# Two-layer decode block on one core: a tile per half of wq, second-layer softmax ahead of the key turns, value steps re-spaced, last values loaded into key tiles

## The chip, the cores and the metric

The kernel runs on one core of a Trainium2 chip. The metric is the time of one execution on the device in microseconds (us); a profile of one execution gives its span, which is about 1.8 us shorter than the time. The engines are PE (matrix multiply, TensorE), DVE (VectorE), ACT (ScalarE) and SP, which here only issues transfers. All loads go through one queue and are spread over 16 DMA engines.

A run is called fast or slow by its time: slow means over 1.5% above the fastest run of the same kernel. Ratios below are the mean time of one kernel's fast runs over that of the kernel before's fast runs of the same rounds, so they are not quite the ratios of the medians that are quoted with them. Microseconds worked out from a ratio are (1 - ratio) x 374.8.

## The reference

Batch 4, one new token each, model width 512. A grouped-query attention block (32 query heads, 8 key/value heads, 4096 cached keys, head size 128) and a gated feed-forward block (width 1792) are applied twice, with the **same** weights and the **same** caches both times:

```python
x = A_x
x = x + _A_ref(_layernorm(x), k_cache, v_cache, wq, wo)
x = x + _B_ref(_layernorm(x), w_gate, w_up, w_down)
x = x + _A_ref(_layernorm(x), k_cache, v_cache, wq, wo)
x = x + _B_ref(_layernorm(x), w_gate, w_up, w_down)
# _A_ref: q = x @ wq; p = softmax(q k^T / sqrt(128)); (p v) @ wo
# _B_ref: (gelu(x @ w_gate) * (x @ w_up)) @ w_down
```

All inputs are bf16. Keys and values of one batch entry are 8.4 MB each.

## The kernel before

A batch entry's keys are loaded once, as 16 tiles of 512 KB (`KT`), and serve both layers. A tile has to be transposed by DVE once (a "key turn"). Values are not kept: they are streamed once for each layer through a ring of six slots of 512 KB. So block b does: scores of layer 2 for entry b-1 from the keys that are still there; each key tile is then free and is loaded with entry b's keys; softmax of layer 2 (two head groups); key turns; scores and softmax of layer 1 for entry b; 16 value steps of layer 1; output projection; the dense stage (feed-forward, next queries) into which the 16 value steps of layer 2 for entry b-1 are woven. One value step is 16 matmuls on one value tile, and it frees the tile's slot.

```python
KV_BUFS = 6
wq_sb = wts.tile([P, KD, HqDh], BF16, name="wq_sb")         # both head groups in one tile
KT = [[wts.tile([P, CH, Dh], BF16, ...) for t in range(NT)] for i in range(Hkv)]

def load_v(upto):                                            # values go through the ring alone
    while seen["load"] < min(upto * VB, seen["use"] + KV_BUFS):
        ...
        v = kvin.tile([P, CH, Dh], BF16, name="v_t", tag="kv")
        dq.dma_start(out=v[:], in_=cache_tile(A_v_cache, plan[i][0], kvh, t))

# in attend(b2, b1), blocks two to four:
for g in range(NG):
    for t in range(NT):
        scores(sc2[g], g, t)
        keys.load(GH)
p0 = soft(sc2[0]); build_q1(b1, 0)
turn()                                                       # waits for the first key tile
z0 = soft_turn(*p0); prob2[0] = (soft_swap(p0[0], p2p), z0)
p0 = soft(sc2[1]); build_q1(b1, 1)
turn()
z0 = soft_turn(*p0); prob2[1] = (soft_swap(p0[0], p2p), z0)
turn(2)
# ... 5 more turns and the first score half ...
turn(2); vals.step(2); sc1 = new_scores(); scores(sc1, 1, 0)
turn(4); vals.step(2); scores(sc1, 1, 1); vals.step(2)       # and so on
# (cut: dense(), attend_last(), the first block)
```

An instruction that waits holds up what stands behind it in the program on the same engine: in the trace below, one wait of 15.1 us on PE holds up all later matmuls, and the key turns on DVE with them.

Of the kernel before, what the change touches and what calls it, by code (L numbers as in the profile page):

```python
# [29 lines left out]
def kernel(  # L30
# [50 lines left out]

    dq = nc.sync

    wq_sb = wts.tile([P, KD, HqDh], BF16, name="wq_sb")
    wo_sb = wts.tile([P, Hq, D], BF16, name="wo_sb")
    wg_sb = wts.tile([P, KD, F], BF16, name="wg_sb")
    wu_sb = wts.tile([P, KD, F], BF16, name="wu_sb")
# [26 lines left out]

    def load_wq(g):
        n = HG * Dh
        dq.dma_start(out=wq_sb[:, :, g * n:(g + 1) * n], in_=wq_dram[:, :, g * n:(g + 1) * n])

    def load_rest():
        n = Hq // 4  # L120
# [72 lines left out]
    def turn_rows(rows, n):  # L193
        t = tmpp.tile([P, n // QS, QS], FP32, name="rt", tag="row")
        nc.vector.transpose(out=t.rearrange("p n j -> p (n j)"), in_=rows[:, :n])  # L195
        return t

    def q_rows(b0, nb, g):
        bs = slice(b0, b0 + nb)
        rows = new_rows()  # L200
        for k in range(KD):
            for j in range(QD):
                n0 = (g * GH + j) * rep * Dh
                w = wq_sb[:, k, n0:n0 + rep * Dh].rearrange("p (m i e) -> p m e i", i=QS, e=2)
                nc.tensor.matmul(rows[j * QS:j * QS + nb, :], lhsT=xn_bf[:, k, bs], rhs=w,  # L205
                                 start=(k == 0), stop=(k == KD - 1))
        return rows
# [27 lines left out]
    def build_q1(b, g):  # L235
        q_build(q_spread(q1_bf[:, g, :, b], amask, g), g)


    def y_select(rows, nb):
        t = turn_rows(rows, 512).rearrange("p (k a) j -> p a k j", a=QD)  # L240
        y = ps_sm.tile([P, KD, nb], FP32, name="y", tag="sm")
        for a in range(QD):
            nc.tensor.matmul(y[a * QS:(a + 1) * QS], lhsT=s32_f[:, :], rhs=t[:, a, :, :nb],
                             start=True, stop=True)
        return y
# [57 lines left out]
    class Keys:  # L303
# [14 lines left out]
        def turn(self, count=1):  # L318
            for _ in range(count):
                kvh, t = self.tile(self.nt)  # L320
                self.nt += 1
                words = KT[kvh][t].rearrange("p c d -> p (c d)").bitcast(FP32)
                nc.vector.transpose(out=words, in_=words)  # L323
# [33 lines left out]
    def soft_turn(pp, ls):  # L357
        flat = pp.rearrange("p c j -> p (c j)")
        nc.vector.transpose(out=flat, in_=flat)  # L359
        zx = zp.tile([P, GH, rep], FP32, name="zx", tag="zx")  # L360
        nc.vector.tensor_scalar(out=zx[:], in0=dmask[:], scalar1=ls[:, 0:1], scalar2=None,
                                op0=ALU.mult)
        return zx
# [18 lines left out]
    ring = []  # L382
    seen = {"load": 0, "use": 0}

    def load_v(upto):
        while seen["load"] < min(upto * VB, seen["use"] + KV_BUFS):
            i, n = divmod(seen["load"], VB)
            seen["load"] += 1
            kvh, t = divmod(n, NT)
            v = kvin.tile([P, CH, Dh], BF16, name="v_t", tag="kv")  # L390
            dq.dma_start(out=v[:], in_=cache_tile(A_v_cache, plan[i][0], kvh, t))
            ring.append(v)

# [35 lines left out]
    def attend(b2, b1):  # L429
        two, first = b2 is not None, b1 == 0  # L430
        prob1, prob2 = {}, {}
        keys = Keys(b1)
        turn = keys.turn
        vals = Values(b1, 0, prob1, lambda k: OT_bf[:, k * rep:(k + 2) * rep],
                      1 if first else len(plan))
        if two:
            sc2 = [new_scores() for g in range(NG)]
            for g in range(NG):
                for t in range(NT):
                    scores(sc2[g], g, t)  # L440
                    keys.load(GH)
            p0 = soft(sc2[0])
            build_q1(b1, 0)
            turn()
            z0 = soft_turn(*p0)
            prob2[0] = (soft_swap(p0[0], p2p), z0)
            p0 = soft(sc2[1])
            build_q1(b1, 1)
            turn()
            z0 = soft_turn(*p0)  # L450
            prob2[1] = (soft_swap(p0[0], p2p), z0)
            turn(2)
        else:
            load_wq(0)
            keys.load(TG)
            load_wq(1)
            keys.load(TG)
            load_v(1)
            make_identity(nc, ident_bf[:])
            build_consts()  # L460
            xT_ps = ps_sm.tile([P, KD, B], BF16, name="xT_ps", tag="sm")
            for k in range(KD):
                nc.tensor.transpose(xT_ps[:, k, :], x_bf[:B, k * P:(k + 1) * P], ident_bf[:B, :B])
            nc.vector.tensor_copy(out=XX[:, 0].rearrange("p b k -> p k b"), in_=xT_ps[:])
            ln_square(0, B)
            rstd1 = ln_rstd(B, ln_center(0, B))
            q_first(q_rows(0, B, 0), 0, rstd1)
            build_q1(0, 0)
            turn(4)
        sc1 = new_scores()  # L470
        scores(sc1, 0, 0)
        turn(4)
        scores(sc1, 0, 1)
        if first:
            q_first(q_rows(0, B, 1), 1, rstd1)
            build_q1(0, 1)
        turn()
        p0 = soft(sc1)
        turn()
        z0 = soft_turn(*p0)  # L480
        prob1[0] = (soft_swap(p0[0], p1p), z0)
        turn(2)
        vals.step(2)
        sc1 = new_scores()
        scores(sc1, 1, 0)
        turn(4)
        vals.step(2)
        scores(sc1, 1, 1)
        vals.step(2)
        p0 = soft(sc1)  # L490
        vals.step()
        z0 = soft_turn(*p0)
        vals.step()
        prob1[1] = (soft_swap(p0[0], p1p), z0)
        rows = new_rows()
        hp = 2 * rep
        if first:
            vals.step(TG)
            load_rest()
            load_v(len(plan))  # L500
            out_proj(rows, OT_bf, 0, Hq)
        else:
            for i in range(2):
                vals.step()
                out_proj(rows, OT_bf, i * hp, hp)
            vals.step(3)
            out_proj(rows, OT_bf, 2 * hp, hp)
            vals.step(3)
            out_proj(rows, OT_bf, 3 * hp, hp)
        assert vals.n == VB  # L510
        return rows, prob2

    def attend_last(b2):
        prob2 = {}
        vals = Values(b2, 1, prob2, lambda k: OT2_bf[:, k * rep:(k + 2) * rep, b2])
        sc2 = [new_scores() for g in range(NG)]
        for g in range(NG):
            for t in range(NT):
                scores(sc2[g], g, t)
        for g in range(NG):  # L520
            p0 = soft(sc2[g])
            z0 = soft_turn(*p0)
            prob2[g] = (soft_swap(p0[0], p2p), z0)
            vals.step(2)
        vals.step(6)
        rows = new_rows()
        hp = 2 * rep
        for i in range(2):
            vals.step()
            out_proj(rows, OT2_bf, i * hp, hp)  # L530
        vals.step(3)
        out_proj(rows, OT2_bf, 2 * hp, hp)
        vals.step(3)
        out_proj(rows, OT2_bf, 3 * hp, hp)
        return rows

    def dense(b0, nb, rows, fill):
        y = y_select(rows, nb)
        fill(2)
        add_y(b0, nb, y)  # L540
        ln_square(b0, nb)
        mv = ln_center(b0, nb)
        fill(1)
        rg = ffn_in(b0, nb, wg_sb)
        rstd = ln_rstd(nb, mv)
        sq, h = gelu(nb, rg, rstd)
        ru = ffn_in(b0, nb, wu_sb)
        H_bf = gate_up(nb, sq, h, ru)
        fill(3)
        y = y_select(down(nb, H_bf), nb)  # L550
        add_y(b0, nb, y)

    x_bf = tmpp.tile([P, D], BF16, name="x_bf", tag="row")
# [3 lines left out]
    for b in range(B):  # L557
        fill = (lambda n: None) if prev is None else prev.step
        dense(b, 1, rows, fill)
        fill(2)  # L560
        ln_square(b, 1)
        mv = ln_center(b, 1)
        fill(2)
        rstd = ln_rstd(1, mv)
        am = small.tile([P, QD], FP32, name="am", tag="am")
        nc.vector.tensor_scalar(out=am[:], in0=amask[:], scalar1=rstd[:, 0:1], scalar2=None,
                                op0=ALU.mult)
        qr = [q_rows(b, 1, g) for g in range(NG)]
        for g in range(NG):
            qm = q_spread(turn_rows(qr[g], 512)[:, :, 0], am, g)  # L570
            fill(2)
            q_build(qm, g)
        fill(VB)
        if b < B - 1:
            rows, prob2 = attend(b, b + 1)
            prev = Values(b, 1, prob2, lambda k, b=b: OT2_bf[:, k * rep:(k + 2) * rep, b])
        else:
            rows = attend_last(b)
# [41 lines left out]
```

## Time and profile before

374.75 us, median of three runs (373.92 to 376.08). The page of the profiled run, first its busy line, then, of the rows in 40 equal slices, the mean busy share of the DMA engines in tenths and what they moved, then the load queue's packets, bytes and share:

```profile
PE 216.0 (58%) x3522; PEld 114.2 (31%) x3522; DVE 173.5 (46%) x476; ACT 24.2 (6%) x54; POOL 0.7 (0%) x6
...
DMA  7999428999929969998999599899993999996900
GB/s 277 398 409 406 192 99 304 372 366 386 390 88 368 410 233 343 359 322 299 337 407 410 180 300 396 299 336 354 413 409 129 333 384 356 319 339 180 375 17 0
...
q1 hardware_dynamic: 35744, 114.58, 83.7%
```

The kernel moves 114.6 MB. Its best slices run at 405 to 413 GB/s, at which these bytes would take about 280 us (worked out: 114.6 MB / 0.41 MB per us). The other 95 us are slices in which the queue moves less. No engine that computes is near full over the span. The Trainium skill, "Perfetto Trace Analysis", Roofline, says that a lone core's HBM rate is bounded by its 16 DMA engines at about 435 GB/s.

Windows of the trace in which the queue had little it was allowed to fetch (window, its length, busy time of each engine, granted clock, DMA busy share, GB/s):

```profile
42.00:53.00 11.00, 3.26 (x63) 2.41 (x67) 9.53 (x17) 2.65 (x4) 0.00 (x0) 0.63 0.03 9
104.00:110.00 6.00, 4.57 (x62) 1.71 (x58) 3.07 (x9) 0.00 (x0) 0.00 (x0) 0.81 0.05 17
206.00:212.00 6.00, 3.30 (x62) 2.23 (x65) 6.00 (x9) 1.00 (x3) 0.00 (x0) 0.50 0.23 87
282.00:288.00 6.00, 3.03 (x62) 2.17 (x65) 6.00 (x8) 1.27 (x3) 0.00 (x0) 0.50 0.12 46
336.00:342.00 6.00, 2.79 (x84) 1.98 (x77) 3.05 (x10) 2.17 (x6) 0.00 (x0) 0.98 0.32 104
```

Idle on the queue is the bottleneck's idle time here. The first row alone is 11 us. The queue's own waits say what for: the value loads (L391) waited 146.5 us in 75 waits for PE's value steps to free a slot.

```profile
SPq L391 <- PE ot L418: 146.5, 75, 14.9
```

Why the first of these windows: in the time line (start, duration, engine, line, operation, out<-in, count, and in brackets the idle time before and what ended it) the first query projection starts with four matmuls at 9.16 us and then stands still for 15 us, for a wq load, although its own half of wq had landed. DVE turns the first key only behind it.

```profile
9.16 0.60 PE L205 MATMUL rows<-wq_sb,xn_bf 128*4 128x512 bf16 x4 [4.36 <-DMA wq_sb<-in_A_wq_dram]
...
24.89 1.45 PE L205 MATMUL rows<-wq_sb,xn_bf 128*4 128x512 bf16 x12 [15.14 <-DMA wq_sb<-in_A_wq_dram]
...
28.34 9.12 DVE L323 STREAM_TRANSPOSE kt<-kt 128x1024 f32<-128x1024 f32 x8
```

The third block, DVE: the second query build, then 5.18 us of idle time until the first key lands, then softmax work between the turns:

```profile
183.77 0.42 DVE L229 TENSOR_TENSOR qb<-qe,amask 128x256 bf16<-128x256 f32 x1 [0.34 <-PE qe L226]
189.38 1.25 DVE L323 STREAM_TRANSPOSE kt<-kt 128x1024 f32<-128x1024 f32 x1 [5.18 <-DMA kt<-in_A_k_cache_dram]
...
191.24 0.68 DVE L340 TENSOR_REDUCE m<-sc 128x1 f32<-128x512 f32 x1
...
195.31 8.00 DVE L323 STREAM_TRANSPOSE kt<-kt 128x1024 f32<-128x1024 f32 x7
```

The time line of SP alone divides the span. A block's *key stage* runs from its first key issue to its first value issue, its *value stage* from there to the next block's first key issue:

```profile
108.87 15.76 SPq L316 DMA_DIRECT2D kt<-in_A_k_cache_dram  x16
134.13 45.55 SPq L391 DMA_DIRECT2D v_t<-in_A_v_cache_dram  x32
180.25 18.43 SPq L316 DMA_DIRECT2D kt<-in_A_k_cache_dram  x16
210.48 45.22 SPq L391 DMA_DIRECT2D v_t<-in_A_v_cache_dram  x32
257.19 17.81 SPq L316 DMA_DIRECT2D kt<-in_A_k_cache_dram  x16
286.75 63.35 SPq L391 DMA_DIRECT2D v_t<-in_A_v_cache_dram  x42
```

The end, on PE: the last 64 score matmuls, and the value step that waited last for a value. They are 26.3 us apart (start to start).

```profile
330.82 5.78 PE L334 MATMUL sc<-kt,qb 128*32 128x512 bf16 x64
...
357.07 0.58 PE L418 MATMUL ot<-pe,v_t 128*128 128x4 bf16 x16 [0.68 <-DMA v_t<-in_A_v_cache_dram]
```

### The profile page before, as it was taken

Reading aid. Unit: us, or ns where it says so; the run is one execution under the profiler, and the core shown is the slowest. Engines: PE = TensorE matmul, PEld = TensorE weight load, DVE = VectorE, ACT = ScalarE, POOL = GpSimd, SP = SyncE. Lnnn points to the kernel's source line nnn. Section 1 sums busy time; section 2 is a strip of 40 time slices with the busy share of each in tenths; the row PEclk is TensorE's granted clock in tenths of the full one; section 3 lists DMA queues with packets and bytes.
Section 4 is the critical chain, followed back from the end, with each engine's and each line's share of the span. In section 5 each row is a group of like instructions: output and inputs, shape, how many; then the busy total and the mean of one; then the engine's idle time right before and its main releaser. Section 6 shows DMA issues by size and latency. Waiting matters only on the chain.

```text
span 374.5 us, 8051 instructions
## 1 busy us (share of the span) xinstructions
PE 216.0 (58%) x3522; PEld 114.2 (31%) x3522; DVE 173.5 (46%) x476; ACT 24.2 (6%) x54; POOL 0.7 (0%) x6
## 2 busy tenths in 40 slices
PE   1015465334472587688625685887075778885564
PEld 0001134301121145445201353553013445535231
DVE  5019582004268972245279821552599315523033
ACT  0000111000002001000020110000101100002000
POOL 0000000000000000000000000000000000000000
PEclk9999855555587555556855555666555556667555
DMA  7999428999929969998999599899993999996900
GB/s 277 398 409 406 192 99 304 372 366 386 390 88 368 410 233 343 359 322 299 337 407 410 180 300 396 299 336 354 413 409 129 333 384 356 319 339 180 375 17 0
DMA packets 35779, 115.09 MB, mean 307 GB/s; under 512 B 3224, under 2 KB 9120, under 8 KB 35744
## 3 DMA queue, kind: packets, MB, share of 16 engines
q1 hardware_dynamic: 35744, 114.58, 83.7%
q8 instruction: 27, 0.44, 0.5%
q14 instruction: 8, 0.07, 0.1%
HBM read 114.56 MB, written 0.00 MB: 306 GB/s over the span
## 4 chain that ended last, share of the span: by engine, by line
DVE 34%; DMA 32%; PE 23%; SPq 4%; issue 4%; ACT 2%; ACTq 0%
DVE kt L323 17%; DMA v_t<-in_A_v_cache_dram 15%; DMA kt<-in_A_k_cache_dram 8%; PE sc L334 6%; PE ot L418 6%; DMA wd_sb<-in_B_w_down_dram 5%; DMA wq_sb<-in_A_wq_dram 4%; DVE rt L195 3%; SPq L122 3%; DVE pp L359 3%; DVE m L340 2%; PE rows L254 2%; PE rows L298 2%; PE rows L205 2%; PE ot L410 1%
## 5 line engine op out<-in xcount | busy, mean ns | idle before, releaser
L418 PE MATMUL ot<-pe,v_t 128*128 128x4 bf16 x2048 | 67.2, 166 | 34.6 <-DMA v_t<-in_A_v_cache_dram 22.0
L418 PEld LDWEIGHTS <-v_t 128*128 128x128 bf16 x2048 | 62.9, 104 | 60.2 <-DMA v_t<-in_A_v_cache_dram 29.8
L323 DVE STREAM_TRANSPOSE kt<-kt 128x1024 f32<-128x1024 f32 x64 | 74.4, 1211 | 9.8 <-DMA kt<-in_A_k_cache_dram 9.8
L334 PE MATMUL sc<-kt,qb 128*32 128x512 bf16 x512 | 63.5, 556 | 11.9 <-DVE kt L323 11.3
L195 DVE STREAM_TRANSPOSE rt<-rows 128x512 f32<-128x512 f32 (+1 forms) x30 | 20.8, 693 | 59.4 <-PE rows L205 25.6
L370 PE MATMUL x<-pp,ident_bf 128*32 128x128 bf16 x256 | 9.3, 287 | 47.2 <-DVE pp L359 47.2
L423 DVE TENSOR_TENSOR OT_bf<-ot,rden 128x8 bf16<-128x8 f32 x32 | 5.3, 165 | 66.2 <-PE ot L418 62.0
L334 PEld LDWEIGHTS <-qb 128*32 128x32 bf16 x512 | 18.2, 119 | 44.8 <-issue 38.1
L205 PE MATMUL rows<-wq_sb,xn_bf 128*1 128x512 bf16 (+1 forms) x160 | 18.1, 607 | 20.0 <-DMA wq_sb<-in_A_wq_dram 19.5
L254 PE MATMUL rows<-wo_sb,OT_bf 128*1 128x512 bf16 (+1 forms) x160 | 20.5, 609 | 9.2 <-DMA wo_sb<-in_A_wo_dram 8.2
L370 PEld LDWEIGHTS <-ident_bf 128*32 128x32 bf16 x256 | 6.5, 120 | 50.8 <-issue 41.4
L340 DVE TENSOR_REDUCE m<-sc 128x1 f32<-128x512 f32 x16 | 10.9, 683 | 21.9 <-PE sc L334 21.9
L353 ACT ACTIVATE pp<-sc,nm 128x512 bf16<-128x512 f32 x16 | 11.0, 688 | 150.4 <-DVE junk L349 150.4
L359 DVE STREAM_TRANSPOSE pp<-pp 128x512 bf16<-128x512 bf16 x16 | 11.0, 688 | 6.6 <-ACT pp L353 6.6
L205 PEld LDWEIGHTS <-xn_bf 128*1 128x1 bf16 (+1 forms) x160 | 4.7, 112 | 29.1 <-issue 27.8
L373 ACT CAST pe<-x 128x512 bf16<-128x512 f32 x16 | 9.4, 586 | 40.0 <-PE x L370 40.0
L298 PE MATMUL rows<-wd_sb,H_bf 128*1 128x512 bf16 (+1 forms) x70 | 7.7, 523 | 4.6 <-DMA wd_sb<-in_B_w_down_dram 3.5
L268 PE MATMUL rows<-wu_sb,xn_bf 128*1 128x448 bf16 (+1 forms) x80 | 8.5, 576 | 3.0 <-DMA wu_sb<-in_B_w_up_dram 3.0
L410 PE MATMUL ot<-zx,mean_f 128*128 128x16 f32 x32 | 9.5, 376 | 0.0
L229 DVE TENSOR_TENSOR qb<-qe,amask 128x256 bf16<-128x256 f32 x16 | 6.8, 422 | 5.8 <-PE qe L226 5.8
L268 PE MATMUL rows<-wg_sb,xn_bf 128*1 128x448 bf16 (+1 forms) x80 | 8.3, 567 | 1.9 <-DVE r L176 1.3
L410 PEld LDWEIGHTS ot<-zx,mean_f 128*128 128x128 f32 x32 | 8.0, 309 | 1.7 <-issue 1.6
(61 smaller groups left out, 91.6 us busy)
## 6 DMA issues: line engine op xcount, KB each, us to landing
v_t<-in_A_v_cache_dram SPq DMA_DIRECT2D x128, 512.0 KB, 7.4
kt<-in_A_k_cache_dram SPq DMA_DIRECT2D x64, 512.0 KB, 10.3
wq_sb<-in_A_wq_dram SPq DMA_DIRECT2D x2, 2048.0 KB, 8.0
wo_sb<-in_A_wo_dram SPq DMA_DIRECT2D x4, 1024.0 KB, 12.2
wg_sb<-in_B_w_gate_dram SPq DMA_DIRECT2D x1, 1792.0 KB, 13.5
wu_sb<-in_B_w_up_dram SPq DMA_DIRECT2D x1, 1792.0 KB
wd_sb<-in_B_w_down_dram SPq DMA_DIRECT2D x1, 1792.0 KB, 18.8
x_bf<-in_A_x_dram SPq DMA_DIRECT2D x1, 4.0 KB
```

Of the source, the lines that this page charges most:

```text
L195: nc.vector.transpose(out=t.rearrange("p n j -> p (n j)"), in_=rows[:, :n])
L205: nc.tensor.matmul(rows[j * QS:j * QS + nb, :], lhsT=xn_bf[:, k, bs], rhs=w, start=(k == 0), stop=(k == KD - 1))
L254: nc.tensor.matmul(rows[r0:r0 + nb, :], lhsT=lhsT, rhs=wo_sb[:, i, :], start=(i < QD), stop=(i >= Hq - QD))
L268: nc.tensor.matmul(rows[j * QS:j * QS + nb, :KF * QS], lhsT=xn_bf[:, k, bs], rhs=w[:, j], start=(k == 0), stop=(k == KD - 1))
L298: nc.tensor.matmul(rows[r0:r0 + nb, :], lhsT=H_bf[:, c, :], rhs=wd_sb[:, c, :], start=(c < QD), stop=(c >= KF - QD))
L323: nc.vector.transpose(out=words, in_=words)
L334: nc.tensor.matmul(sc[s * QS:(s + 1) * QS], lhsT=QB[g][:, w0:w0 + 2 * W], rhs=kt[:, :, be // 2, :, be % 2], start=(t == 0 and be == 0), st ...
L340: nc.vector.tensor_reduce(out=m[:], in_=sc.rearrange("p c j -> p (c j)"), axis=AX.X, op=ALU.max)
L359: nc.vector.transpose(out=flat, in_=flat)
L370: nc.tensor.matmul(x[a * QS:(a + 1) * QS, s], lhsT=ident_bf[:, s * QS:(s + 1) * QS], rhs=pT[:, a], start=True, stop=True, skip_group_check ...
L410: nc.tensor.matmul(self.ot[:, 1], lhsT=mean_f[:, :], rhs=zx[:], start=True, stop=True, skip_group_check=True)
L418: nc.tensor.matmul(self.ot[:, 0, s], lhsT=v[:, i, :], rhs=pe[:, s, c, :], start=(c == 0), stop=(c == C - 1), skip_group_check=True)
```

## The change

Four parts, all of them order and placement; no bytes and no arithmetic are added or removed.

1. **wq**: a tile for each head group, so that the first group's matmuls need not wait for the second group's load. The second group's query build in the first block moves behind four more key turns.
2. **Softmax order**: in blocks two to four both second-layer softmaxes stand ahead of the key turns.
3. **Value steps**: spread more evenly over the score halves and the dense stage.
4. **Last values**: at the end the key tiles are dead, so the last ten value tiles are loaded there instead of through the ring. The same edit moves the first group's last softmax ahead of the second group's scores and re-spaces the value steps there.

```diff
-    wq_sb = wts.tile([P, KD, HqDh], BF16, name="wq_sb")
+    wq_sb = [wts.tile([P, KD, HG * Dh], BF16, name=f"wq_sb{g}") for g in range(NG)]
 ...
-    def load_v(upto):
-        while seen["load"] < min(upto * VB, seen["use"] + KV_BUFS):
+    def load_v(upto, free=()):
+        free = list(free)
+        while seen["load"] < upto * VB and (free or seen["load"] < seen["use"] + KV_BUFS):
 ...
-            v = kvin.tile([P, CH, Dh], BF16, name="v_t", tag="kv")
+            v = free.pop(0) if free else kvin.tile([P, CH, Dh], BF16, name="v_t", tag="kv")
 ... attend(), blocks two to four
-            p0 = soft(sc2[0])
-            build_q1(b1, 0)
-            turn()
-            z0 = soft_turn(*p0)
-            prob2[0] = (soft_swap(p0[0], p2p), z0)
-            p0 = soft(sc2[1])
-            build_q1(b1, 1)
-            turn()
-            z0 = soft_turn(*p0)
-            prob2[1] = (soft_swap(p0[0], p2p), z0)
-            turn(2)
+            for g in range(NG):
+                p0 = soft(sc2[g])
+                build_q1(b1, g)
+                z0 = soft_turn(*p0)
+                prob2[g] = (soft_swap(p0[0], p2p), z0)
+            turn(4)
 ... attend(), all blocks
-        if first:
-            q_first(q_rows(0, B, 1), 1, rstd1)
-            build_q1(0, 1)
         turn()
         p0 = soft(sc1)
         turn()
         z0 = soft_turn(*p0)
         prob1[0] = (soft_swap(p0[0], p1p), z0)
         turn(2)
+        if first:
+            q_first(q_rows(0, B, 1), 1, rstd1)
+            build_q1(0, 1)
         vals.step(2)
         sc1 = new_scores()
         scores(sc1, 1, 0)
         turn(4)
-        vals.step(2)
+        vals.step(3)
         scores(sc1, 1, 1)
-        vals.step(2)
+        vals.step(1)
 ... attend_last()
-        for g in range(NG):
-            for t in range(NT):
-                scores(sc2[g], g, t)
+        for t in range(NT):
+            scores(sc2[0], 0, t)
+            free += [KT[s][t] for s in range(GH)]
+        p0 = soft(sc2[0])
+        for t in range(NT):
+            scores(sc2[1], 1, t)
+            free += [KT[GH + s][t] for s in range(GH)]
+        load_v(len(plan), free)
 ... dense() and the query stage behind it
-        y = y_select(rows, nb)
-        fill(2)
+        y = y_select(rows, nb, fill)          # one step inside it
         add_y(b0, nb, y)
         ln_square(b0, nb)
+        fill(1)
         mv = ln_center(b0, nb)
         fill(1)
         rg = ffn_in(b0, nb, wg_sb)
         ...
+        fill(1)
         ru = ffn_in(b0, nb, wu_sb)
 ... (the rest of the same kind is left out)
```

More of the change, by code (lines that the diff above doesn't have):

```diff
@@ L116, in load_wq @@
         n = HG * Dh
-        dq.dma_start(out=wq_sb[:, :, g * n:(g + 1) * n], in_=wq_dram[:, :, g * n:(g + 1) * n])
+        dq.dma_start(out=wq_sb[g][:], in_=wq_dram[:, :, g * n:(g + 1) * n])
     def load_rest():
@@ L202, in q_rows @@
             for j in range(QD):
-                n0 = (g * GH + j) * rep * Dh
-                w = wq_sb[:, k, n0:n0 + rep * Dh].rearrange("p (m i e) -> p m e i", i=QS, e=2)
+                n0 = j * rep * Dh
+                w = wq_sb[g][:, k, n0:n0 + rep * Dh].rearrange("p (m i e) -> p m e i", i=QS, e=2)
                 nc.tensor.matmul(rows[j * QS:j * QS + nb, :], lhsT=xn_bf[:, k, bs], rhs=w,
@@ L236, in build_q1, with y_select @@
         q_build(q_spread(q1_bf[:, g, :, b], amask, g), g)
-    def y_select(rows, nb):
+    def y_select(rows, nb, fill):
         t = turn_rows(rows, 512).rearrange("p (k a) j -> p a k j", a=QD)
+        fill(1)
         y = ps_sm.tile([P, KD, nb], FP32, name="y", tag="sm")
@@ L486, in attend @@
         turn(4)
-        vals.step(2)
+        vals.step(3)
         scores(sc1, 1, 1)
-        vals.step(2)
+        vals.step(1)
         p0 = soft(sc1)
-        vals.step()
+        vals.step(1)
         z0 = soft_turn(*p0)
-        vals.step()
+        vals.step(1)
         prob1[1] = (soft_swap(p0[0], p1p), z0)
@@ L515, in attend_last @@
         vals = Values(b2, 1, prob2, lambda k: OT2_bf[:, k * rep:(k + 2) * rep, b2])
+        free = []
         sc2 = [new_scores() for g in range(NG)]
-        for g in range(NG):
-            for t in range(NT):
-                scores(sc2[g], g, t)
-        for g in range(NG):
-            p0 = soft(sc2[g])
-            z0 = soft_turn(*p0)
-            prob2[g] = (soft_swap(p0[0], p2p), z0)
-            vals.step(2)
-        vals.step(6)
+        for t in range(NT):
[6 more added lines that the diff above has]
+        load_v(len(plan), free)
+        z0 = soft_turn(*p0)
+        prob2[0] = (soft_swap(p0[0], p2p), z0)
+        p0 = soft(sc2[1])
+        vals.step(3)
+        z0 = soft_turn(*p0)
+        prob2[1] = (soft_swap(p0[0], p2p), z0)
+        vals.step(5)
         rows = new_rows()
@@ L546, in dense @@
         sq, h = gelu(nb, rg, rstd)
+        fill(1)
         ru = ffn_in(b0, nb, wu_sb)
@@ L549, in dense @@
         fill(3)
-        y = y_select(down(nb, H_bf), nb)
+        y = y_select(down(nb, H_bf), nb, fill)
         add_y(b0, nb, y)
@@ L559 @@
         dense(b, 1, rows, fill)
+        ln_square(b, 1)
         fill(2)
-        ln_square(b, 1)
         mv = ln_center(b, 1)
-        fill(2)
+        fill(1)
         rstd = ln_rstd(1, mv)
@@ L567 @@
                                 op0=ALU.mult)
-        qr = [q_rows(b, 1, g) for g in range(NG)]
-        for g in range(NG):
-            qm = q_spread(turn_rows(qr[g], 512)[:, :, 0], am, g)
-            fill(2)
-            q_build(qm, g)
+        qr0 = q_rows(b, 1, 0)
+        fill(1)
+        qm0 = q_spread(turn_rows(qr0, 512)[:, :, 0], am, 0)
+        qr1 = q_rows(b, 1, 1)
+        fill(1)
+        q_build(qm0, 0)
+        qm1 = q_spread(turn_rows(qr1, 512)[:, :, 0], am, 1)
+        fill(2)
+        q_build(qm1, 1)
         fill(VB)
```

## The prediction

It was written from the profile of the kernel before alone, with nothing of the change built.

> **What bounds the kernel now.** It moves 114.6 MB, and the DMA queue table gives the queue 83.7% of the span. In stretches with a full queue the windows view shows 405 to 420 GB/s, so the same bytes need about 280 us of the 374.5. The Trainium skill, "Perfetto Trace Analysis", Roofline, puts a lone core's ceiling at about 435 GB/s, set by its 16 DMA engines; this trace agrees (at most 422 in a 2 us window). So the kernel is bound by DMA plus stretches in which the queue has nothing it may fetch: 42 to 53 us, 104 to 110, 133 to 135, 207.5 to 211.5, 283 to 288, 337 to 341 and 357 to the end. Only shortening those, or the thin stretches (200 to 330 GB/s) behind the six value slots, can help.
>
> **1. wq tile per group (firm).** The second to fourth contraction steps of the first query projection wait until 24.9 us: they wait for the second wq load, which overlaps theirs in one tile, although their own data landed at 9.2. Eight key tiles were in SBUF, untouched. With two tiles the first key turns start near 13 instead of 28.3 and become bound by key arrival (1.28 us a tile; a turn takes 1.15). First values are used near 36 instead of 51, just when the first of them land, so the idle 42 to 53 and the thin stretch to 62 go. Values should end landing near 56 instead of 71.7, wd near 82 instead of 97.8. Gain 15.5 us (14 to 16.5).
>
> **2. Second-layer softmax ahead of turns.** In 189.4 to 195.4 VectorE spends 3.7 us on softmax and query build, after sitting idle 5.2 us for the first key. Moved into that idle time they are free; then turns are arrival-bound, so about 2.7 us remain per period for the second and third period. In the first (113 us) the idle time is only 0.8 us: gain about 0.7. Sum 6 us.
>
> **3. Value steps spread.** Three values before the second score half (was two) and one, not two, around it free slots earlier; dense-stage windows of 205 to 290 GB/s (240 to 248, 168 to 172, 318 to 322) should fill. I count 2 to 3 us for each of three periods: 8 us. This is the least certain term, since the thin rates appear even while DMA engines show busy.
>
> **4. Last values into key slots (firm).** At the end the queue idles 337 to 341 and then feeds ten tiles through six slots until 356.5. Continuous fetch ends near 349.5: gain 7 to 9, say 8. The 14 us tail of the last dense stage stays.
>
> Matmul, turn and softmax counts and durations are unchanged; nothing is added except reordering.
>
> **Sum.** 15.5 + 6 + 8 + 8 = 37.5, so 337 us; range 328 to 350. Faster by over 2%: 0.97; within 2%: 0.025; slower: 0.005.
>
> **What would show it.** Bytes unchanged; mean DMA rate about 340 GB/s. wd lands by 80 to 84. First key turn near 13 us. In the later periods VectorE does no softmax between the first key's landing and the first eight turns, and the queue idles under 2 us before the values. Periods (first key issue to first key issue) shrink from 77 and 75.5 to about 71. The last value lands 13 to 14 us after the last scores start, not 26. The chain of waits becomes more DMA and less key turns.
>
> **What would make it wrong.** The first values ring-limited after all (step 1 worth 12); value fetches staying thin at 300 GB/s with six slots, so steps 2 and 3 only move the wait; a step placed before a short VectorE chain holding TensorE on a value not landed, lengthening the dense chain.

## The result and the profile after

Four runs: 345.83 to 350.54 us, median 346.9, against 374.77 before; ratio 0.927 (95% interval 0.920 to 0.934). A later set of six runs on another chip gave 0.923 (0.916 to 0.930). That is 27 to 29 us faster, inside the stated range and about 10 us short of the point. The page of the profiled run (345.83 us, the fastest of its set):

```profile
PE 217.3 (63%) x3522; PEld 114.0 (33%) x3522; DVE 175.3 (51%) x476; ACT 24.2 (7%) x54; POOL 0.7 (0%) x6
...
DMA  7999999999579889999999689999997989999800
GB/s 260 411 406 396 405 386 334 352 403 372 217 236 409 333 288 309 380 327 381 373 415 407 244 289 407 367 356 347 412 409 255 321 319 407 396 336 370 343 4 0
...
q1 hardware_dynamic: 35744, 114.58, 89.7%
```

The same bytes, the same work on each engine; the emptiest slices of the queue went. Among the queue's own waits, the value loads' wait for free slots fell from 146.5 to 103.3 us (the second line, waits that ended with an earlier value's landing, is compared further down):

```profile
SPq L393 <- PE ot L420: 103.3, 72, 8.3
...
SPq L393 <- DMA v_t<-in_A_v_cache_dram: 17.2, 25, 3.5
```

The first block (time line of PE and of DVE): all 16 matmuls of the first query projection go at 9.07 us and the first turn at 12.94, not 28.34. Eight turns later DVE waits for a key, so it has caught up with the loads.

```profile
9.07 1.88 PE L205 MATMUL rows<-wq_sb,xn_bf 128*4 128x512 bf16 x16 [4.27 <-DMA wq_sb<-in_A_wq_dram]
...
12.94 9.12 DVE L324 STREAM_TRANSPOSE kt<-kt 128x1024 f32<-128x1024 f32 x8
25.98 1.25 DVE L324 STREAM_TRANSPOSE kt<-kt 128x1024 f32<-128x1024 f32 x1 [3.92 <-DMA kt<-in_A_k_cache_dram]
```

The third block, DVE: the softmax of both groups is over at 173.86, 8.2 us after the block's first key issue, when the first key is there; no softmax stands between the turns, and the eighth of them waits 0.42 us for its key.

```profile
172.69 0.42 DVE L229 TENSOR_TENSOR qb<-qe,amask 128x256 bf16<-128x256 f32 x1 [0.30 <-PE qe L226]
...
173.86 8.12 DVE L324 STREAM_TRANSPOSE kt<-kt 128x1024 f32<-128x1024 f32 x7
182.40 2.50 DVE L324 STREAM_TRANSPOSE kt<-kt 128x1024 f32<-128x1024 f32 x2 [0.42 <-DMA kt<-in_A_k_cache_dram]
```

SP's time line, and the end on PE (the last score matmuls and the last waited-for value are now 22.7 us apart):

```profile
95.23 15.87 SPq L317 DMA_DIRECT2D kt<-in_A_k_cache_dram  x16
120.27 44.33 SPq L393 DMA_DIRECT2D v_t<-in_A_v_cache_dram  x32
165.70 17.08 SPq L317 DMA_DIRECT2D kt<-in_A_k_cache_dram  x16
191.95 43.32 SPq L393 DMA_DIRECT2D v_t<-in_A_v_cache_dram  x32
236.76 17.05 SPq L317 DMA_DIRECT2D kt<-in_A_k_cache_dram  x16
262.97 42.90 SPq L393 DMA_DIRECT2D v_t<-in_A_v_cache_dram  x32
307.36 10.65 SPq L393 DMA_DIRECT2D kt<-in_A_v_cache_dram  x10
```

```profile
305.45 5.07 PE L335 MATMUL sc<-kt,qb 128*32 128x512 bf16 x64
...
328.12 0.59 PE L420 MATMUL ot<-pe,kt 128*128 128x4 bf16 x16 [0.66 <-DMA kt<-in_A_v_cache_dram]
```

Taking the differences of these starts divides the 30.4 us between the two profiled spans (gains from the unrounded times):

| stage | before, us | after, us | gain |
|---|---|---|---|
| first block, to the second block's first key issue | 108.9 | 95.2 | 13.6 |
| second block (71.4 = 25.3 key + 46.1 value) | 71.4 | 70.5 | 0.9 |
| third block (30.2 + 46.7) | 76.9 | 71.1 | 5.9 |
| fourth block (29.6 + 44.1, to the last scores) | 73.6 | 68.7 | 4.9 |
| end | 43.7 | 38.6 | 5.0 |

The windows of the changed kernel that answer to those shown before, and two of another kind at the end:

```profile
90.00:96.00 6.00, 4.57 (x62) 1.65 (x58) 3.29 (x10) 0.00 (x0) 0.00 (x0) 1.00 0.12 46
118.00:122.00 4.00, 2.62 (x50) 1.54 (x49) 4.00 (x6) 0.36 (x1) 0.00 (x0) 0.50 0.36 129
190.00:194.00 4.00, 2.67 (x48) 1.38 (x48) 4.00 (x5) 0.04 (x1) 0.00 (x0) 0.50 0.38 126
260.00:266.00 6.00, 4.62 (x98) 2.93 (x91) 6.00 (x7) 0.58 (x1) 0.00 (x0) 0.50 0.58 188
308.00:312.00 4.00, 2.67 (x56) 1.27 (x52) 2.20 (x8) 0.78 (x2) 0.00 (x0) 1.00 0.97 288
222.00:228.00 6.00, 4.67 (x90) 3.25 (x82) 2.31 (x12) 0.00 (x0) 0.00 (x0) 0.50 0.98 309
```

The idle windows are shorter (before the third block's values 4.0 x 0.62 = 2.5 us are left of 6.0 x 0.77 = 4.6), and the last two rows show what the prediction took too lightly: DMA engines that count as busy for 97 to 98% of the time and move 288 to 309 GB/s. The Trainium skill, "Perfetto Trace Analysis", Identifying the Most-Contended Engine, says that for DMA occupancy misleads and HBM utilization (throughput) should be used instead; these two rows are a case of it.

The granted TensorE clock was 0.62 of full speed before and 0.69 after. It isn't the cause: a run below with the softmax order alone had 0.695 and gained under 1%, and eleven executions of the kernel before, in the rounds of the runs below, had 0.609 to 0.704 and took 371.2 to 376.7 us, the slowest of them at 0.692.

### The profile page after: what moved, and what is told of

Read it like the earlier page. It is cut to its first block, busy times and chain, and to the rows that moved or that the text cites. A ratio compares the mean times of both kernels' runs of the same rounds, so it can differ in the third digit from the quotient of the medians.

```text
span 344.1 us, 8051 instructions
## 1 busy us (share of the span) xinstructions
PE 217.3 (63%) x3522; PEld 114.0 (33%) x3522; DVE 175.3 (51%) x476; ACT 24.2 (7%) x54; POOL 0.7 (0%) x6
## 4 chain that ended last, share of the span: by engine, by line
DMA 46%; PE 27%; DVE 18%; SPq 5%; issue 3%; ACT 1%; ACTq 0%
DMA v_t<-in_A_v_cache_dram 18%; DMA kt<-in_A_k_cache_dram 17%; DVE kt L324 7%; PE sc L335 7%; PE ot L420 7%; DMA kt<-in_A_v_cache_dram 6%; DMA wd_sb<-in_B_w_down_dram 5%; PE rows L205 3%; PE rows L269 3%; SPq L122 3%; PE rows L255 2%; DVE rt L195 2%; DVE pp L360 2%; PE rows L299 2%; DVE m L341 2%
## 5 line engine op out<-in xcount | busy, mean ns | idle before, releaser
L420 PE MATMUL ot<-pe,v_t 128*128 128x4 bf16 x1888 | 63.1, 167 | 28.1 <-DMA v_t<-in_A_v_cache_dram 15.7
L420 PEld LDWEIGHTS <-v_t 128*128 128x128 bf16 x1888 | 58.6, 105 | 58.1 <-issue 31.4
L335 PE MATMUL sc<-kt,qb 128*32 128x512 bf16 x512 | 62.4, 552 | 18.0 <-DVE kt L324 18.0
L371 PE MATMUL x<-pp,ident_bf 128*32 128x128 bf16 x256 | 8.4, 266 | 32.1 <-DVE pp L360 32.1
L205 PE MATMUL rows<-wq_sb,xn_bf 128*1 128x512 bf16 (+1 forms) x160 | 18.7, 620 | 4.7 <-DMA wq_sb<-in_A_wq_dram 4.3
L299 PE MATMUL rows<-wd_sb,H_bf 128*1 128x512 bf16 (+1 forms) x70 | 8.6, 572 | 4.7 <-DMA wd_sb<-in_B_w_down_dram 3.5
L226 PE MATMUL qe<-qm,t_bf 128*128 128x64 bf16 x16 | 3.4, 214 | 9.2 <-DVE qm L216 9.2
## 6 DMA issues: line engine op xcount, KB each, us to landing
wg_sb<-in_B_w_gate_dram SPq DMA_DIRECT2D x1, 1792.0 KB, 13.6
```

What stands on the lines that cost most here:

```text
L205: nc.tensor.matmul(rows[j * QS:j * QS + nb, :], lhsT=xn_bf[:, k, bs], rhs=w, start=(k == 0), stop=(k == KD - 1))
L299: nc.tensor.matmul(rows[r0:r0 + nb, :], lhsT=H_bf[:, c, :], rhs=wd_sb[:, c, :], start=(c < QD), stop=(c >= KF - QD))
L335: nc.tensor.matmul(sc[s * QS:(s + 1) * QS], lhsT=QB[g][:, w0:w0 + 2 * W], rhs=kt[:, :, be // 2, :, be % 2], start=(t == 0 and be == 0), st ...
L371: nc.tensor.matmul(x[a * QS:(a + 1) * QS, s], lhsT=ident_bf[:, s * QS:(s + 1) * QS], rhs=pT[:, a], start=True, stop=True, skip_group_check ...
L420: nc.tensor.matmul(self.ot[:, 0, s], lhsT=v[:, i, :], rhs=pe[:, s, c, :], start=(c == 0), stop=(c == C - 1), skip_group_check=True)
```

## The experiments

Theory A: the load queue is the bottleneck; what gates it is when slots and key tiles come free. The four parts act in different stages and add. What is missing from the predicted 37.5 us is missing because the six slots keep the queue too shallow to run at its full rate. Rivals, per run, stand in the expectations.

### The four parts alone, on the kernel before

`e1_wq` has part 1 alone (the wq and `q_first` lines of the diff above), `e2_soft` part 2, `e3_steps` part 3, `e4_last` part 4. `e1_tile` is part 1 without moving the query build:

```diff
# e1_tile: wq in two tiles, and this stays where it was
         scores(sc1, 0, 1)
         if first:
             q_first(q_rows(0, B, 1), 1, rstd1)
             build_q1(0, 1)
```

> The kernel before with wq in two tiles and the second group's query build moved after four more key turns, nothing else. Theory A (stages gate the load queue one after another, so the parts add): the first keys of the second block are issued 13.6 us earlier than in the kernel before (95.2 against 108.9 us), everything behind is unchanged, total 13 to 14 us less than before (ratio about 0.964). Rival B (the early gain is partly taken back or partly owed to other parts): 8 us or less, or over 18.

> The kernel before with wq in two tiles but the second group's query build left where it was. Theory A: the tile alone gives 12 to 14 us, as values land no earlier than 36 us and the later query build is hidden behind that. Rival B: the move is a large part, and the tile alone gives under 10 us.

> The kernel before with the second-layer softmax of both groups ahead of the key turns, nothing else. Theory A: only the second and third key stages shorten, by 3 to 4 us each (first key issue to first value issue 30.2 and 29.6 us before, 26.3 and 26.2 in the changed kernel), the first by under 0.5; total 6.5 to 8 us less (ratio about 0.981). Rival B: the value stages behind are bound by DMA packets and give it back, total under 3 us.

> The kernel before with the value steps and dense reordering alone. Theory A: the value stages (first to last value issue 45.6, 45.2 and about 43 us before; 44.3, 43.3 and 42.9 in the changed kernel) shorten by 1 to 2 us each, total 3 to 5 us less (ratio about 0.989). My prediction said 8. Rival B: the value stages are set by slow packets, not by free slots, and the total is within 1.5 us of before.

> The kernel before with the last values loaded into freed key tiles alone. Theory A: only the end changes, by the 5.0 us by which the end is shorter in the changed kernel (43.6 to 38.6 us from the last scores' start), ratio about 0.987. My prediction said 8. Rival B: the end also needed the other parts, under 3 us here.

| run | median, us | ratio (95% interval) | worked out, us |
|---|---|---|---|
| e1_wq | 361.28 | 0.966 (0.962 to 0.971) | 12.7 less |
| e1_tile | 360.79 | 0.965 (0.961 to 0.968) | 13.2 less |
| e2_soft | 370.59 | 0.991 (0.986 to 0.996) | 3.5 less |
| e3_steps | 370.08 | 0.990 (0.985 to 0.996) | 3.6 less |
| e4_last | 371.55 | 0.993 (0.987 to 0.998) | 2.8 less |

The wq tile is the large part, and the tile alone is all of it; moving the query build gives nothing that can be measured. The second block's keys were issued at 95.09 us in `e1_wq` (theory A: 95.2) and at 94.73 in `e1_tile`, here on its SP time line:

```profile
94.73 15.64 SPq L316 DMA_DIRECT2D kt<-in_A_k_cache_dram  x16
```

The other three gains are clear of zero but under 2% of the time. `e3_steps` is within what theory A said. `e2_soft` is not: 6.5 to 8 us were expected, and its interval ends at 5.4. `e4_last` gained what its rival B said (under 3), not the 5.0 of theory A, though its interval (0.7 to 4.8 us) nearly reaches that.

The parts sum to 22.6 us, the whole change gives 27 to 29. The small parts' intervals are about 2 us each way, so the 5 us between may be interplay or noise; that isn't settled. The profiled run of `e4_last` was slow, so its stages aren't used.

### One part taken out of the changed kernel

```diff
# a_nosteps: the changed kernel with part 3 undone; a_nosoft: with part 2 undone
```

> The changed kernel with the value steps and dense order of before. Theory A: 3 to 5 us slower than the changed kernel, the same as the part alone gains. Rival B: under 1.5 us (the value stages shortened for another reason).

> The changed kernel with the softmax order of before (a key turn inside each of the two second-layer softmaxes). The four parts alone came to about 22.5 us by their ratios, the whole change to 27 or 28. Theory A (the softmax order shortens the key stages by 3.2 us twice whatever stands behind, but alone part of it was given back in the value stages, as their slots did not come free earlier): 5 to 8 us slower than the changed kernel (ratio to before 0.938 to 0.947). Rival B (the parts add, the difference is noise): 2.5 to 4.5 us slower (0.931 to 0.937).

`a_nosteps`: 350.56 us, ratio 0.938 (0.935 to 0.942), so against the changed kernel's 0.927 (or 0.923) part 3 is worth 4 to 6 us in the whole. `a_nosoft`: 352.41 us, 0.937 (0.932 to 0.943), so part 2 is worth 4 to 5 us. This lies between what theory A (5 to 8) and the rival (2.5 to 4.5) had said of `a_nosoft`, and doesn't decide between interplay and noise.

Stages from SP's time lines pool several fast profiled runs, which says more than one run's total. In the third and fourth block the key stage took 25.8 to 27.6 us in the four runs with the new softmax order and six slots (the changed kernel twice, `e2_soft`, `a_nosteps`; mean 26.6) and 27.9 to 30.2 us in the five with the old (before, `e1_wq`, `e1_tile`, `e3_steps`, `a_nosoft`; mean 29.5): 2.9 us a block, 5.9 us for both, and under half a microsecond in the second block (25.3 to 25.1 in the means). So the mechanism is as predicted, to its size (6 us). The total gains only about 4 us. In `e2_soft` the value stage of the fourth block gave some back (45.6 us, against 44.1 before), but the other runs with the old steps spread from 44.1 to 44.9 there, so where the rest went is not shown.

With the new value steps the value stages of blocks two, three and four took 45.7, 44.7 and 42.8 us (means of the changed kernel twice, `e3_steps`, `a_nosoft`), with the old 46.2, 46.3 and 44.8 (before, `e1_wq`, `e1_tile`, `e2_soft`, `a_nosteps`): 0.6, 1.7 and 2.1 (from the unrounded means), sum 4.3 us of the 8 predicted. The 0.6 is not clear of noise: the runs with the new steps spread from 43.7 to 47.6 us in the second block. A value stage moves about 32 tiles, which at 410 GB/s is 41 us (worked out), so it stood 4 to 5 us above that.

The end (last scores' start to the last instruction) took 41.6 to 43.7 us in the five runs with the old end and 37.0 to 39.2 in six with the new (the changed kernel twice, `a_nosteps`, `a_nosoft` and the two runs of the last group below): 42.6 against 38.0 in the mean, so 4.6 us of the 8 predicted.

### Is the queue too shallow? Five slots, and seven

```diff
# a_ring5
-KV_BUFS = 6
+KV_BUFS = 5
```

> The changed kernel with five value slots, not six (seven do not fit in SBUF). Theory A (the queue idles and runs thin because slots are not free): each of about four idle stretches (90, 118, 190 and 261 us) grows by one tile's time, 1.3 us, and the value stages thin further: 6 to 15 us slower than the changed kernel. Rival B (thin stretches come from slow packets whatever the slots): under 3 us slower.

355.21 us, ratio 0.951 (0.947 to 0.955): about 9 us slower than the changed kernel, the size that theory A said. Of the queue's own waits, those of the value loads that ended with an earlier value's landing were 25.4 us, against 17.2 and 22.5 in the two profiled runs of the changed kernel; those for PE's steps stayed about the same in sum (102.6 against 103.3 and 98.0):

```profile
SPq L393 <- PE ot L420: 102.6, 80, 8.3
SPq L393 <- DMA v_t<-in_A_v_cache_dram: 25.4, 46, 4.8
```

But it was not lost where theory A said. The idle stretches ahead of the values did not grow by a tile's time; this is the one of the third block, which moved 126 GB/s with six slots (190 to 194 us above):

```profile
193.00:197.00 4.00, 2.62 (x50) 1.65 (x50) 4.00 (x6) 0.46 (x1) 0.00 (x0) 0.50 0.38 127
```

The value stages grew instead: 48.7, 46.0 and 47.2 us, against 45.4, 44.8 and 42.5 (and 47.6, 44.6 and 43.4 in the second profiled run) with six slots.

Seven slots were counted not to fit as the kernel stands (a slot is 4 KB a partition). The room was made by sharing:

```diff
# a_ring7
-KV_BUFS = 6
+KV_BUFS = 7
-    p1p = ... bufs=NG          # the first group's probabilities are used up when the second's are made
+    p1p = ... bufs=1
-    grp = ... bufs=2
+    grp = ... bufs=1
-    zp  = ... bufs=2 * NG + 1
+    zp  = ... bufs=2 * NG
-    mean_f = const.tile([P, P], FP32, ...)      # lhsT=mean_f[:, :]
+    mean_f = const.tile([P, 1], FP32, ...)      # lhsT=mean_f[:, 0:1].broadcast_to([P, P])
-        pp = tmpp.tile(..., tag="pp")
+        pp = tmpp.tile(..., tag="row")          # shares the 2 KB of the turned rows
# and OT_bf in OT2_bf's column b1, xoT in xn_bf, H_bf in h, hv and msq in r2, am in mv
```

`after2` is the changed kernel unaltered, for the same chip and rounds.

> The changed kernel again, unaltered, so that it has the same chip and rounds as the next two. Both theories: ratio to the kernel before within 0.920 to 0.934, as in its first four runs (0.927).

> The changed kernel with seven value slots; room for it was made by sharing small tiles, one buffer fewer in three small pools, and a one-column constant read with stride zero. Theory A (the missing gain lies in a load queue that is too shallow: traces so far show 330 GB/s with two to three tiles outstanding and about 400 with five or more; five slots cost 8 to 9 us): 3 to 7 us faster than the changed kernel, the stretches with two to three tiles outstanding fewer. Rival B (slow packets for another reason, or the shared buffers add waits): within 2 us of it, or slower.

`after2`: 348.28 us, 0.923 (0.916 to 0.930). `a_ring7`: **339.56 us, 0.903 (0.897 to 0.908)**, correct. The intervals are apart: this version is about 2.2%, 7.7 us, faster than the changed kernel and beats both. (The rule for slow leaves out three of the six runs of `after2` and two of `a_ring7`; with all of them the means are 347.8 and 339.7, which says the same. The profiled run of `a_ring7` was a slow one, so its stages aren't compared.) The sharing was not run with six slots. It could only be a rival if it saved time itself, which was not tested; with the loss from five slots, the slot is the likelier cause. The Trainium skill, "Perfetto Trace Analysis", Optimization Strategy, says that a gap that keeps repeating on the engine that should be saturated can mean too little SBUF for the next tile. Slots were indeed worth time here, but the repeating gaps at 118, 190 and 261 us are not shown to be of that kind: with one slot fewer they stayed as they were.

How the rate goes with the depth of the queue can be counted from the packet records: for each 1 us of blocks two to four, the tiles issued by SP and not yet loaded, and the bytes moved. Nine fast runs with six slots, pooled (the changed kernel twice, before, `e1_wq`, `e1_tile`, `e2_soft`, `e3_steps`, `a_nosteps`, `a_nosoft`). In the first and third column a tile counts until its last packet ends, in the second for 1.5 us more, which is about when its landing is signalled:

| tiles outstanding | value stages: us counted, GB/s | value stages, to the signal | key stages |
|---|---|---|---|
| 1 to 2 | 47, 296 | 26, 99 | 73, 245 |
| 2 to 3 | 356, 330 | 75, 270 | 37, 365 |
| 3 to 4 | 552, 337 | 345, 325 | 42, 398 |
| 4 to 5 | 219, 344 | 522, 343 | 60, 375 |
| over 5 | 10, 316 | 227, 364 | 476, 390 |

In the value stages the queue mostly holds two to five tiles. Below two it moves less. Above two, the rise with their number is small or clear depending on how a tile is counted (in the second column a tile that has just been moved still counts, so a fast stretch looks deep), so how far depth alone sets the rate is not settled. What is clear is that something else matters too. With the same number outstanding, if it is over two, value stages move less than key stages (first against third column). And with two to three and three to four tiles outstanding, the four runs with the new value steps moved 342 and 351 GB/s in the value stages, the five with the old ones 323 and 326.

The packets themselves show where the rate goes. All packets of keys and values are 4 KB, and the median one took 159 to 160 ns in both kinds of stage. But in the value stages 7 to 8% of them took over 250 ns, and these made up 16 to 20% of all packet time; in the key stages it was 2 to 4% of the packets and 5 to 8% of the time. So a busy but thin queue is here one with a minority of slow packets. What makes them slow stays open.

The Trainium skill, "SBUF — State Buffer", The DMA setup-cost knee, gives each transfer a roughly fixed cost of about 2 us besides its bytes, mostly for completion. This case agrees: hardly a tile's first packet came sooner than 0.6 us after its issue, and its landing was signalled 1.4 to 1.8 us after its last packet (medians of the nine runs). A slot is held for that time too, but no run here isolates what it costs.

### Can the first value steps come earlier?

In the changed kernel two key turns stand between the first layer-1 softmax and the first two value steps, and the queue idles just then. Two variants, for blocks two to four:

```diff
# a_early                      # a_turn1
-        turn(2)               -        turn(2)
         vals.step(2)          +        turn()
+        turn(2)                        vals.step(2)
                               +        turn()
```

> The changed kernel with the first two value steps ahead of the two key turns before them in blocks two to four (VectorE makes the reciprocal for them before, not after, those turns). Theory A: slots are freed 2 us earlier while the queue idles, so each of the three idle stretches (118 to 122, 190 to 194, 261 to 265 us) shrinks by 1.5 to 2 us; total 4 to 6 us less than the changed kernel. Rival B: the second score half then starts later, or the value stages behind are bound elsewhere, and the gain is under 1.5 us.

> The changed kernel with one key turn before and one after the first two value steps in blocks two to four (both were before). Theory A: slots are freed 1.1 us earlier in each of three idle stretches without VectorE waiting for the reciprocal's matmul (in the version with both turns after, it waited 1.1 us and the later turns slipped): 2 to 3 us faster than the changed kernel. Rival B: the value stage behind takes back what the key stage gives, within 1.5 us of it.

Neither is shown to help. `a_early`: 350.9 us, 0.936 (0.932 to 0.940), no faster than the changed kernel's 0.927 and 0.923. DVE now waited 1.14 us for the matmul behind the reciprocal that the value steps need, and the turns behind it slipped. `a_turn1`: 347.01 us, 0.925 (0.920 to 0.930), no different from `after2`; with these two intervals a gain of the 2 to 3 us that theory A said could hardly be told from none. Its key stages did shorten (23.6, 24.3 and 25.8 us against 25.0, 25.8 and 26.2), and its value stages were 46.8, 45.4 and 44.1 against 47.6, 44.6 and 43.4. A slot freed earlier is filled earlier, but in the third and fourth block the values behind it took 0.8 and 0.7 us longer, as rival B has it. That is one profiled run of each, and two runs of the changed kernel differ by as much (43.4 and 42.5 us in the fourth block).

## Why the prediction was right, and where it was off

The direction, the mechanism of each part and the range were right. The size was 37.5 us predicted against 27 to 29 measured, and the difference lies in these terms:

- **Step 1, wq tile: 15.5 predicted, 12.7 to 13.6 measured.** The first turn at 12.9 us and the idle window's end came as said. The down projection's weights were waited for until 84.2 us (said: 82). Of the missing 2 us, about 1.5 (worked out against 410 GB/s) are between 50 and 56 us, where the queue moved 334, 238 and 351 GB/s in three windows of 2 us: the last value slots came free only behind the second softmax (value steps resume at 49.7 us). The prediction named this as a risk ("ring-limited after all, step 1 worth 12").
- **Step 2, softmax order: 6 predicted, 5.9 in the key stages**, about 4 in the total. Right as a stage, partly lost behind it.
- **Step 3, value steps: 8 predicted, about 4 measured.** The prediction had the windows of 205 to 290 GB/s "fill". They filled in part: with two to four tiles outstanding the value stages moved 342 to 351 GB/s with the new steps, against 323 to 326 with the old, and not the 405 to 420 that it took for a full queue.
- **Step 4, last values: 8 predicted, 4.6 in the stage** (2.8 in the run with it alone). In part the same error: the fetch went on without a pause, as said, but at 244 to 332 GB/s from 308 to 312 us, and tailed off over the last 3 us (59 GB/s in 326 to 328 us). And in part the tail: in the second profiled run the last packet ended 19.3 us after the last scores' start, not 22.2, but what stands behind it then took 18.0 us, not 16.4, so the end was only 1.3 us shorter. Besides, "13 to 14 us after the last scores start" contradicted the prediction's own sum, which had the fetch end near 349.5 us, 18.7 us after them; 22.7 us was measured.
- "The queue idles under 2 us before the values": 2.5 us were left in the third block. Blocks of "about 71 us": 70.5, 71.1 and 68.7.

So one idea was wrong in two terms, the third and in part the fourth: time in which a queue is free to fetch was taken as time at its full rate. The risk was written down ("value fetches staying thin at 300 GB/s with six slots"), but the sum didn't hold it. Of theory A's last claim, that the missing time is owed to a queue that six slots keep too shallow, the worth of a slot is shown, but not the way in which it acts.

## What to carry to other kernels

When loads bound a kernel, look at its DMA windows for two different faults, an idle queue and a busy but thin one. Reordering shortened the first here. The second gave way a little to the spacing of the steps and, as far as shown, to buffer space: the version with 4 KB a partition more for a seventh slot gained 7.7 us, more than moving the softmax or spacing the steps did. Give separately loaded pieces of a weight separate tiles, since a wait can be for the whole tile's later load: that was the largest gain for the smallest edit. And cost freed loading time at the rate that the queue shows in *that* stage, not at its best rate.

## What the Trainium skill lacked or had wrong

- "DMA: Bandwidth & Descriptors", Bandwidth, gives rate by size of a transfer (up to 425 GB/s at 16 MB), but not by how many transfers are outstanding. Here 512 KB tiles moved 330, 337 and 344 GB/s in the value stages with 2 to 3, 3 to 4 and 4 to 5 of them outstanding, and 390 in key stages with over five.
- "Perfetto Trace Analysis", What "DMA-bound" means, lists engines, the issuing sequencer and SBUF reads, but not too few buffers to load into: one value slot fewer cost about 9 us, and the version with one more gained 7.7 us of 347. (The same page's remark on repeating gaps and SBUF space comes nearest, but the gaps that repeat here did not grow with one slot fewer.)
- No page that was read says why, among packets of one size, 7 to 8% take over 250 ns in the value stages (median 159 ns) and 2 to 4% in the key stages; it stays open here too.
